# The first batch's last expert becomes the first slot of the second stage, its weights made in small pieces

## The chip, the core and the metric

The kernel runs on one core of one Trainium2 chip. The metric is the device time of one execution in microseconds (us); the figure for the kernel before is the median of three timed runs. A profile of one further execution shows where the time goes.

## The reference, cut to what matters

```
attn_out = attention(q, k, v, centroids)          # 4 batches, 8 heads, 768 rows, 64 wide
x = attn_out as [3072, 512]                       # 768 rows of each batch
P = balanced gates exp(x @ w_gate), 8 experts
for e in range(8):
    h = maximum(x @ w1[e], 0)                     # [3072,512] @ [512,1024]
    out += P[:, e:e+1] * (h @ w2[e])              # [3072,1024] @ [1024,512]
```

Only the mixture of experts is touched by the change; attention stands ahead of it and stays as it is.

## The kernel before, in words

**Two precisions.** Each fp32 matrix is split into a high and a low fp16 part, and each product is made of three matmuls (high by high, high by low, low by high). The first matrix product of an expert (`layer1`) is done with seven products in place of eight (Strassen's scheme in Winograd's form), 42 matmuls of 384 columns for a **quarter** of an expert, which is 256 of its 1024 hidden columns. An expert has four quarters. The weights of the seven products are four sums and three plain parts of `w1`, each in a high and a low part; they are made once and stored in DRAM (`w1d`).

**First stage: batch 0, 32 blocks.** The loop `for t in range(NI)` goes over the 8 x 4 quarters; I call one turn a *block* t. A block has seven steps m = 0 to 6. Each step makes one product of `layer1`, and from step 1 on one row tile of `layer2` of the quarter before: six matmuls of 512 columns, that is, the second matrix product in its plain form, 36 matmuls for a quarter. While block t runs, `make_w` makes the weights of quarter t+1 from the raw ones: ScalarE (ACT) scales and makes high parts, GpSimd (POOL) makes the four sums and the low parts of `w1`, VectorE (DVE) the low parts of `w2` (`second_matrix`, L1502). `scan` takes magnitudes of a later expert's raw weights for its scale. `store_w` writes the made weights to DRAM. The results of layer 2 collect in six PSUM tiles over the four blocks of an expert; `gated` adds them to `acc`, one 128x512 DVE instruction a tile (L1562), in the block after the expert's last one. Those blocks (t = 4, 8, 12, ...) I call *heavy*.

**Second stage: batches 1 to 3, 24 slots.** A *slot* is one expert of one batch, 28 steps. `layer1b` makes the first products, and `layer2b` the second products of the slot before, which here too are seven products in place of eight: 252 matmuls of 256 columns. The first slot has only `layer1b`, seven steps a quarter. The four sums of `w2` that the seven products need are made in the second stage's first eight slots: `load_second` (tile `r`), `second_sums` on POOL (`s2w`), `second_high` on ACT, `second_low` on DVE, with a store to `w2d`. `load_left` loads them back (tile `w2o`). `evict` gates results into the totals C11, C12, C21, C22 and X; at a batch's last expert POOL adds X to C12 and C22 (L1821), and the totals are stored as output.

**What sets the order.** Each engine executes its instructions in the order of the program. In the second stage a table of times (`at`, `plan_slot`) says in which step an instruction is issued; `keep_order` pins it. The engine that evicts matters to TensorE (PE): layer 1 has two PSUM tiles in turn, and a product can begin only when DVE or ACT has read what its tile held. In a block, what product 6 leaves must be read (L1401, tile `c`) before step 1 of the next block, which comes after one product only, since step 0 has no layer 2.

**Reload of x.** The seven input matrices of a batch's layer 1 (`xsB..`, `xsT..`, 384 KB each) have one buffer each. At a batch's last quarter `reload_x` loads the next batch's matrix as soon as the product that used the old one is done (L1381). All loads and stores that matter here are issued by SyncE (SP), one queue, in program order.

Of the kernel before, what the change touches and what calls it, by code (L numbers as in the profile page):

```python
# [22 lines left out]
P = 128  # L23
# [141 lines left out]
def attn_moe_kernel(  # L165
# [1116 lines left out]
    ps_h = pool("ps_h", 2, space=PSUM)  # L1282

    def h_tile():
        return ps_h.tile([P, 512], F32, name="h_ps")
# [35 lines left out]

    def spread_powers(am, n, name, use):

        d = dram.tile([P, n], F32, name=name)
        nc.sync.dma_start(out=d, in_=am)
        yield
        t = gs.tile([P, P, n], F32, name=f"all{n}", bufs=1)
# [126 lines left out]
    next(sink)  # L1454
    before = iter(())

    with ExitStack() as ax:
        hc = pool("hc", 4, ax)
        hp = pool("hp", 2, ax)
        wbp = pool("wbp", 3, ax)  # L1460
        sump = pool("sump", 1, ax)
        junkp = pool("junkp", 1, ax)
        rawp = pool("rawp", 8, ax)
        accp = pool("accp", 1, ax)
        ps_o = pool("ps_o", 6, ax, space=PSUM)
# [26 lines left out]
        def first_matrix(idx):  # L1492
            raw = raws[idx][:, 0:1024]
            return raw, raw.rearrange("p (k c t f) -> p t k c f", k=2, c=KC, t=2), sump.tile([P, 4, KC, P], F32, name="s1w")

# [35 lines left out]

        def store_w(idx, wt):
            e, f2 = divmod(idx, NP2)
            wa, wb = wt
            if idx > 1:
                nc.sync.dma_start(out=w1d[idx], in_=wa.rearrange("p x a c f -> p (x a c f)"))
            for o, t, h in ((A22, 0, 1), (A11, 1, 0), (A12, 0, 0)):
                nc.sync.dma_start(out=w2d[e][:, o, f2], in_=wb[:, :, t, h * HD : (h + 1) * HD])
# [14 lines left out]

        def gated(e, acc):
# [12 lines left out]

        AHEAD = 7
        wts = {}
# [7 lines left out]
        plan.unpin()  # L1577
        acc = accp.tile([P, NT, DO], F32, name="acc")
        scans = {i - 5: (i,) for i in range(8, NI)}
        loads = {0: (), 1: (4, 5), 2: (6, 7, 8), 3: (9, 10)}  # L1580
        loaded = {}
        for t in range(NI):
            e, f2 = divmod(t, NP2)
            if f2 == 0:
                po = []
            for idx in loads.get(t, (t + AHEAD,) if t + AHEAD < NI else ()):
                load_raw(idx)
            if 0 < t < NI - 1:
                wts[t + 1] = w_tiles()
                making = make_w(t + 1, wts[t + 1])  # L1590
            if t + 2 >= NI:
                loaded[t + 2] = load_wa((t + 2) % NI)
# [31 lines left out]
            for m in range(7):  # L1624
# [23 lines left out]
            wts.pop(t - 1, None)  # L1648
            before = layer2(po, hh, hl, wt, f2 == 0, f2 == NP2 - 1, gated(e, acc) if f2 == NP2 - 1 else None)
        for x in (sink, inputs, scanning):  # L1650
            for _ in x:
                pass
# [12 lines left out]
    hop = pool("hop", 6)  # L1665
    accp = pool("accb", 1)
    ps_y = pool("ps_y", 1, space=PSUM)
    slots = [(b, e) for b in range(1, B) for e in range(E)]
    NS = len(slots)
# [62 lines left out]
    def plan_slot(n):  # L1732
# [22 lines left out]
        at(base - 1, gate_slot, n)  # L1755
        if b == 1:
            first = base - SLOT
# [9 lines left out]
    LAST = {3: ("C11", 0, 0), 4: ("C22", 1, 1), 5: ("C12", 0, 1), 6: ("C21", 1, 0)}  # L1767
    totals = {}

    def evict(e, ps, gates_, into, begun, qs):  # L1770
        for q in qs:
            for name, j in into:
                t, gate = totals[name][:, q], gates_[:, 3 * j + q : 3 * j + q + 1]
                if e == 0 and (name, q) not in begun:
                    begun.add((name, q))
                    nc.vector.tensor_scalar(out=t, in0=ps[q], scalar1=gate, scalar2=None, op0=ALU.mult)
                else:
                    nc.vector.scalar_tensor_tensor(out=t, in0=ps[q], scalar=gate, in1=t, op0=ALU.mult, op1=ALU.add)

    def layer2b(n):  # L1780
# [6 lines left out]
        for i, (a, o) in enumerate(ORDER2):  # L1787
# [8 lines left out]
            for name, j in INTO[i]:  # L1796
                if name not in totals:
                    totals[name] = accp.tile([P, 3, HD], F32, name=name, bufs=2 if name == "C21" else 1)
            count = 0
            for g in range(2):  # L1800
                h = parts_.pop((n, g, o))
                for q in range(3):
                    steps = [(h_, w_, f) for f in range(2) for h_, w_ in ((0, 0), (0, 1), (1, 0))]
                    for s_, (h_, w_, f) in enumerate(steps):
# [100 lines left out]
```

## Time and profile before

| | |
|---|---|
| median of three timed runs | 2281.86 us (2281.69 to 2282.4) |
| the profiled execution's own time | 2279.16 us |
| its span, first to last instruction | 2277.1 us |
| attention, until the first block | 477.29 us |
| first stage (32 blocks and their rest) | 477.29 to 955.03 us |
| second stage (24 slots and their rest) | 955.03 to the end |
| granted TensorE clock, mean | 0.995 |

The profile lists for every engine its instructions with start, duration and what ended an idle time before them. Times in it are microseconds from the first instruction. A group of matmuls is shown with the time from its first start to its last (modelled) end, so the lengths of matmul groups that follow each other overlap a little; the distance of their starts is what counts.

### The profile page before, as it was taken

The page shows a single profiled execution, that of the slowest core. Times are in us where ns is not written, and L with a number is a line of the kernel's source. Part 1 is how long each engine was busy: PE and PEld are TensorE (multiplying, and loading weights), DVE is VectorE, ACT ScalarE, POOL GpSimd, SP SyncE. Part 2 cuts the span into 40 slices and gives each one's busy share as a digit, 9 for nine tenths or more (in the row PEclk, how much of TensorE's full clock was granted, in tenths as well). Part 3 has the DMA queues.
Part 4 walks back from the last instruction along what each step waited for, and adds up shares of the span by engine and source line. Part 5 has one row for each costly group of instructions (what it writes and reads, how often), then busy time and mean ns, then how long its engine had stood idle before and what let it go on. Part 6 is the DMA issues. An engine that isn't in the chain of part 4 may idle for free.

```text
span 2277.1 us, 39662 instructions
## 1 busy us (share of the span) xinstructions
PE 2236.1 (98%) x15491; PEld 1458.8 (64%) x15491; DVE 1649.1 (72%) x2777; ACT 1143.1 (50%) x2107; POOL 1118.1 (49%) x997
## 2 busy tenths in 40 slices
PE   6999999999999999999999999999999999999999
PEld 3455554445555555567777777777777777777777
DVE  7988878567666766588788877776676666666667
ACT  7777786555666665354444443333433333333333
POOL 3676787854555655276666653233332332322223
PEclk7999999999999999999999999999999999999999
DMA  5345453365555543586766765544444554434433
GB/s 128 88 101 159 103 142 98 124 218 198 186 168 190 190 139 111 203 300 210 223 218 218 239 219 169 176 144 132 151 156 141 182 170 139 131 130 132 138 130 102
DMA packets 226860, 369.78 MB, mean 162 GB/s; under 512 B 73800, under 2 KB 163824, under 8 KB 226160
## 3 DMA queue, kind: packets, MB, share of 16 engines
q1 hardware_dynamic: 226240, 365.67, 50.3%
q8 instruction: 121, 1.98, 0.4%
q10 hardware_dynamic: 432, 1.57, 0.2%
q14 instruction: 67, 0.55, 0.1%
HBM read 272.22 MB, written 80.62 MB: 155 GB/s over the span
## 4 chain that ended last, share of the span: by engine, by line
PE 91%; DVE 6%; ACT 2%; issue 1%; DMA 1%; SPq 0%; DVEq 0%; ACTq 0%
PE h_ps L1387 38%; PE pb L1805 12%; PE pa L1805 8%; PE pc L1805 8%; PE av_ps L1004 4%; PE o_ps L1547 4%; PE o_ps L1549 4%; PE o_ps L1548 4%; PE exp_ps L945 2%; PE max_ps L849 2%; PE exp_ps L946 2%; DVE mrt L853 2%; PE misc_ps L1045 1%; PE misc_ps L630 1%; ACT pe L952 0%
## 5 line engine op out<-in xcount | busy, mean ns | idle before, releaser
L1387 PEld LDWEIGHTS <-wa 128*128 128x128 f16 x5376 | 525.6, 98 | 302.8 <-issue 5.3
L1805 PEld LDWEIGHTS <-ho 128*128 128x128 f16 x5940 | 580.8, 98 | 137.2 <-DVE ho L1700 1.1
L1387 PE MATMUL h_ps<-xsT,wa 128*128 128x384 f16 x3072 | 581.6, 326 | 1.2 <-DVE xsT L324 0.6
L1387 PE MATMUL h_ps<-xsB,wa 128*128 128x384 f16 x2304 | 436.9, 326 | 1.4 <-DVE B L1401 0.6
L1681 POOL TENSOR_TENSOR B<-B,B 128x768 f32<-128x768 f32 x96 | 197.9, 2064 | 468.2 <-DVE ho L1700 426.6
L1700 DVE TENSOR_TENSOR ho<-B,ho 128x768 f16<-128x768 f32 x283 | 348.1, 1230 | 1.6 <-ACT ho L1696 1.6
L1851 ACT ACTIVATE B<-B 128x384 f32<-128x384 f32 x288 | 149.7, 520 | 371.3 <-DVE B L1401 370.0
L1805 PE MATMUL pb<-w2o,ho 128*128 128x256 f16 x2532 | 322.2, 273 | 0.0
L1401 DVE SCALAR_TENSOR_TENSOR u<-h_ps,m 128x384 f32<-128x384 f32 x256 | 141.7, 553 | 243.5 <-PE h_ps L1387 240.7
L1696 ACT CAST ho<-B 128x768 f16<-128x768 f32 x283 | 226.8, 824 | 14.1 <-POOL B L1681 13.4
L970 POOL TENSOR_TENSOR psum<-psum,pe 128x512 f32<-128x512 f32 x160 | 208.1, 1317 | 43.6 <-ACT pe L952 40.3
L853 DVE TENSOR_REDUCE mrt<-max_ps 128x1 f32<-128x512 f32 (+1 forms) x288 | 188.8, 683 | 41.0 <-PE max_ps L849 39.7
L1805 PE MATMUL pc<-w2o,ho 128*128 128x256 f16 x1692 | 215.7, 273 | 0.3
L1805 PE MATMUL pa<-w2o,ho 128*128 128x256 f16 x1692 | 215.1, 273 | 0.0
L1681 POOL TENSOR_TENSOR B<-B,T 128x768 f32<-128x768 f32 x48 | 95.6, 1991 | 206.0 <-DVE ho L1700 206.0
L952 ACT ACTIVATE pe<-exp_ps 128x512 f32<-128x512 f32 x288 | 164.8, 597 | 56.9 <-PE exp_ps L946 51.2
L1411 ACT ACTIVATE m<-h_ps 128x384 f32<-128x384 f32 x128 | 62.6, 489 | 191.6 <-PE h_ps L1387 190.8
L1849 ACT ACTIVATE B<-h_ps 128x384 f32<-128x384 f32 x96 | 47.1, 490 | 211.4 <-PE h_ps L1387 211.4
L1549 PE MATMUL o_ps<-wb,hl 128*128 128x512 f16 x384 | 145.5, 379 | 0.0
L1548 PE MATMUL o_ps<-wb,hh 128*128 128x512 f16 x384 | 145.5, 379 | 0.0
L1547 PE MATMUL o_ps<-wb,hh 128*128 128x512 f16 x384 | 145.5, 379 | 0.0
L1610 ACT ACTIVATE hh<-c 128x384 f16<-128x384 f32 x128 | 66.9, 523 | 143.2 <-DVE c L1401 142.0
(281 smaller groups left out, 3280.8 us busy)
## 6 DMA issues: line engine op xcount, KB each, us to landing
wa<-w1d SPq DMA_DIRECT2D x98, 896.0 KB
w2o<-w2d SPq DMA_DIRECT2D x168, 512.0 KB
raw<-in_moe_w SPq DMA_DIRECT2D x60, 512.0 KB
w1d<-wa SPq DMA_DIRECT2D x30, 896.0 KB
r<-in_moe_w SPq DMA_DIRECT2D x32, 512.0 KB
w2d<-w2s SPq DMA_DIRECT2D x32, 512.0 KB
w2d<-wb SPq DMA_DIRECT2D x96, 128.0 KB
scan<-in_moe_w SPq DMA_DIRECT2D x32, 256.0 KB
```

Of the source, the lines that this page charges most:

```text
L853: nc.vector.tensor_reduce(out=t["mr"][:, i0 : i0 + ni, ni - 1], in_=ps.rearrange("p (x c) -> p x c", x=ni), axis=AX, op=ALU.max)
L952: nc.scalar.activation(pe, ps.rearrange("p (x c) -> p x c", x=ni), AF.Exp, scale=SCALE)
L970: (nc.gpsimd if e == POOL else nc.vector).tensor_tensor(out=st[:, o : o + N0], in0=old[o], in1=part, op=ALU.add)
L1387: nc.tensor.matmul(ps[:, 0:HB], wa[:, w_, a, c, :], x[:, x_, c, :], start=(first and s_ == 0), stop=(s_ == len(steps) - 1), skip_group_che ...
L1547: nc.tensor.matmul(po[i], hh[:, t, ti], wbh[:, t], start=(first and t == 0), stop=False)
L1548: nc.tensor.matmul(po[i], hh[:, t, ti], wbl[:, t], start=False, stop=False)
L1549: nc.tensor.matmul(po[i], hl[:, t, ti], wbh[:, t], start=False, stop=(last and t == 1))
L1681: nc.gpsimd.tensor_tensor(out=t, in0=d[a], in1=d[c], op=ALU.subtract)
L1696: nc.scalar.copy(t[:, 0], blocks[n, g][o])
L1700: nc.vector.tensor_tensor(out=t[:, 1], in0=blocks[n, g][o], in1=t[:, 0], op=ALU.subtract)
L1805: nc.tensor.matmul(ps[q], h[:, h_, f, q * P : (q + 1) * P], w[:, 2 * g + f, w_], start=(first and g == 0 and s_ == 0 and q % 2 == 0), stop ...
L1851: rests.append(lambda: nc.scalar.activation(c, c, AF.Relu))
```

## The change

Batch 0's expert 7 (`STD = E - 1`) leaves the first stage and becomes slot 0 of the second. The first stage has 28 blocks, the second stage 25 slots. What goes with it:

- The four quarters' weights of expert 7 are still made in the first stage, but no longer by `make_w` in the block before. A generator `later` runs one step in every step of blocks from t = 2 on. It loads each half of a quarter (`w1` or `w2`, 512 KB) once for the magnitudes and once more for the weights, and makes each quarter by a fixed list of pieces, one or two a step, 26 steps from quarter to quarter. In that list the four sums are made by DVE (L333, four 128x256 instructions) instead of POOL.
- `acc` is gone: batch 0 now collects in the totals C11 to C22 as the other batches do, so a tile's eviction is two 128x256 DVE instructions in place of one 128x512.
- The reload of x for batch 1, in the last block before, now happens in the last quarter of slot 0.
- In the first stage there are six raw buffers in place of eight, loads go out six blocks ahead in place of seven, and `w2`'s made weights have four buffers in place of three. Output of batch 0 is stored by SP from the totals in slot 1, not by ACT at the end of the first stage.
- X begins anew in slot 0 (`n == 0`), and the adding of X and the stores of the batch's end now happen in slot 1 too.

```diff
+    STD = E - 1
...
-                if e == 0:
-                    nc.vector.tensor_scalar(out=acc[:, i], in0=ps, scalar1=gate, scalar2=None, op0=ALU.mult)
-                else:
-                    nc.vector.scalar_tensor_tensor(out=acc[:, i], in0=ps, scalar=gate, in1=acc[:, i], op0=ALU.mult, op1=ALU.add)
-                if e == E - 1 and i % 2 == 1:
-                    nc.scalar.dma_start(out=out_v[0][:, i - 1 : i + 1], in_=acc[:, i - 1 : i + 1])
+                j, q = divmod(i, 3)
+                for r, name in enumerate((("C11", "C21"), ("C12", "C22"))[j]):
+                    o, y = totals[name][:, q], ps[:, r * HD : (r + 1) * HD]
+                    if e == 0:
+                        nc.vector.tensor_scalar(out=o, in0=y, scalar1=gate, scalar2=None, op0=ALU.mult)
+                    else:
+                        nc.vector.scalar_tensor_tensor(out=o, in0=y, scalar=gate, in1=o, op0=ALU.mult, op1=ALU.add)
...
-        AHEAD = 7
+        AHEAD = 6
...
+        def later():
+            whole = [(e, f2, m) for e in range(STD, E) for f2 in range(NP2) for m in range(2)]
+            todo, ahead, spreads = whole + whole, [], []
...
+                return {
+                    0: [lambda: nc.scalar.activation(t1, t1, AF.Copy, scale=s1[:, e : e + 1])],
+                    2: [lambda: summed(0, 1)],
+                    3: [second_high],
+                    4: [lambda: summed(2, 3)],
+                    5: [plain_high],
+                    6: [lambda: second_low(0)],
+                    7: [lambda: plain_low(0)],
+                    8: [lambda: second_low(1), lambda: nc.scalar.copy(into["wa"][:, 0, 3:7], S_)],
+                    9: [lambda: plain_low(1)],
+                    11: [lambda: sum_low(0), fetch],
+                    12: [lambda: store_second(idx, into["wb"])],
+                    13: [lambda: sum_low(2), fetch],
+                    16: [lambda: store_first(idx, into["wa"])],
+                }
+
+            TURN = 26
...
-        for t in range(NI):
+        for t in range(NB):
...
+                if t > 1:
+                    step(extra)
                 if m:
                     step(before)
                 if m == 1:
                     store_w(t, wt)
-                if t == NI - 1:
-                    reload_x(1, RIGHT[m])
...
-    slots = [(b, e) for b in range(1, B) for e in range(E)]
+    slots = [(0, e) for e in range(STD, E)] + [(b, e) for b in range(1, B) for e in range(E)]
...
-        if b == 1:
+        if n < E:
...
-                if e == 0 and (name, q) not in begun:
+                if (e == 0 or n == 0 and name == "X") and (name, q) not in begun:
```

The first place is SP's queue in the second stage's first slot, around its last quarter. In names, `w2s` are made sums on their way to DRAM, `wa` the weights of layer 1, `w2o` those of layer 2, `r` raw `w2` for the next sums. Before:

```order
L1724 DMA w2d_6452<-w2s 128x4x512
L1343 DMA wa<-w1d_103 128x3584
L1704 DMA w2o<-w2d_6452 128x2048
L1708 DMA r_11459<-in_moe_w 128x2x512
L1708 DMA r_11496<-in_moe_w 128x2x512
L1343 DMA wa<-w1d_104 128x3584
L1704 DMA w2o<-w2d_6452 128x2048
```

And in the changed kernel:

```order
L1854 DMA w2d_6459<-w2s 128x4x512
L1346 DMA wa<-w1d_99 128x3584
L1384 DMA xsB_11030<-xsd1B_6467 128x1536
L1384 DMA xsT_11042<-xsd1T_6468 128x1536
L1384 DMA xsB_11053<-xsd1B_6470 128x1536
L1384 DMA xsT_11068<-xsd1T_6471 128x1536
L1834 DMA w2o<-w2d_6459 128x2048
L1838 DMA r_11073<-in_moe_w 128x2x512
L1384 DMA xsT_11083<-xsd1T_6469 128x1536
L1384 DMA xsT_11095<-xsd1T_6472 128x1536
L1384 DMA xsB_11108<-xsd1B_6473 128x1536
L1838 DMA r_11116<-in_moe_w 128x2x512
```

The seven loads of x now stand behind the store of sums and the load of `wa` of the slot's last quarter, and the loads of `r`, of `w2o` and of the next `wa` stand between or behind them.

The second place is DVE's order in block 16, a heavy one, steps 2 to 4 (`u` and `c` are layer 1's evictions, `xst` a part of the next batch's x, `hl` the low part of h). Before:

```order
L324 SCALAR_TENSOR_TENSOR xst<-tx,sx,xst 128x768
L1562 SCALAR_TENSOR_TENSOR acc<-o_ps,gates,acc 128x512
L1401 SCALAR_TENSOR_TENSOR u_8943<-h_ps,m_8882 128x384
L1613 SCALAR_TENSOR_TENSOR hl<-c,hh 128x384
L1562 SCALAR_TENSOR_TENSOR acc<-o_ps,gates,acc 128x512
L1401 SCALAR_TENSOR_TENSOR c<-h_ps,u_8943 128x384
```

And in the changed kernel, the same steps:

```order
L325 SCALAR_TENSOR_TENSOR xst<-tx,sx,xst 128x768
L333 TENSOR_TENSOR s1x<-rawx 128x256
L333 TENSOR_TENSOR s1x<-rawx,s1x 128x256
L1586 SCALAR_TENSOR_TENSOR C_6542<-o_ps,gates,C_6542 128x256
L1586 SCALAR_TENSOR_TENSOR C_6543<-o_ps,gates,C_6543 128x256
L1404 SCALAR_TENSOR_TENSOR u_9073<-h_ps,m_9004 128x384
L1744 SCALAR_TENSOR_TENSOR hl<-c,hh 128x384
L1586 SCALAR_TENSOR_TENSOR C_6542<-o_ps,gates,C_6542 128x256
L1586 SCALAR_TENSOR_TENSOR C_6543<-o_ps,gates,C_6543 128x256
L1404 SCALAR_TENSOR_TENSOR c<-h_ps,u_9073 128x384
L1658 SCALAR_TENSOR_TENSOR wb<-rawx,s_93,wb 128x512
```

Two sums and one low part of expert 7's weights have come between the evictions, and each eviction of layer 2 is two instructions.

## Rows read from the trace of the kernel before

**Rows 1.** The page: span, busy time by engine, the chain by engine.

```profile
span 2277.1 us, 39662 instructions
...
PE 2236.1 (98%) x15491; PEld 1458.8 (64%) x15491; DVE 1649.1 (72%) x2777; ACT 1143.1 (50%) x2107; POOL 1118.1 (49%) x997
...
PE 91%; DVE 6%; ACT 2%; issue 1%; DMA 1%; SPq 0%; DVEq 0%; ACTq 0%
```

**Rows 2.** Groups of PE's instructions: shape, count, busy, mean ns, idle before.

```profile
L1387 PE MATMUL h_ps<-xsT,wa 128*128 128x384 f16 x3072 | 581.6, 326 | 1.2 <-DVE xsT L324 0.6 <-DVE B L1401 0.4
...
L1805 PE MATMUL pb<-w2o,ho 128*128 128x256 f16 x2532 | 322.2, 273 | 0.0
...
L1549 PE MATMUL o_ps<-wb,hl 128*128 128x512 f16 x384 | 145.5, 379 | 0.0
```

**Rows 3.** Windows: blocks 8 to 27, slots 11 to 15, slot 0.

```profile
core 0: us, PE busy (x) PEld busy (x) DVE busy (x) ACT busy (x) POOL busy (x), PEclk, DMA share, GB/s
596.99:888.88 291.89, 291.89 (x1561) 152.65 (x1560) 189.95 (x314) 182.83 (x303) 160.39 (x164) 1.00 0.50 166
1532.73:1806.78 274.05, 274.05 (x2102) 205.48 (x2100) 184.49 (x310) 105.50 (x177) 82.80 (x43) 1.00 0.47 153
...
955.03:983.68 28.65, 27.69 (x169) 16.42 (x168) 17.97 (x26) 14.90 (x25) 17.61 (x21) 1.00 0.84 284
```

**Rows 4.** Timeline of PE in slot 0: its two waits [idle before <-releaser].

```profile
970.25 1.14 PE L1387 MATMUL h_ps<-xsT,wa 128*128 128x384 f16 x6 [0.36 <-DVE B L1401]
...
982.71 2.11 PE L1387 MATMUL h_ps<-xsB,wa 128*128 128x384 f16 x12 [0.60 <-DVE B L1401]
```

**Rows 5.** Timeline of SP: last reload of x; first and last of seven transfers.

```profile
946.16 0.32 SPq L1381 DMA_DIRECT2D xsB<-xsd1B  x1
...
969.76 0.36 SPq L1724 DMA_DIRECT2D w2d<-w2s  x1
...
978.53 0.46 SPq L1343 DMA_DIRECT2D wa<-w1d  x1
```

**Rows 6.** DMA issues, 930 to 990 us: count and KB each.

```profile
wa<-w1d SPq DMA_DIRECT2D x6, 896.0 KB
...
w2d<-w2s SPq DMA_DIRECT2D x4, 512.0 KB
xsT<-xsd1T SPq DMA_DIRECT2D x4, 384.0 KB
```

**Rows 7.** Windows of slot 0's end: last two columns are DMA share, GB/s.

```profile
970.00:975.00 5.00, 4.75 (x30) 2.86 (x30) 3.20 (x5) 2.48 (x5) 3.65 (x5) 1.00 0.99 315
975.00:980.00 5.00, 5.00 (x32) 3.00 (x31) 2.87 (x4) 4.31 (x8) 1.12 (x3) 1.00 1.04 393
980.00:985.00 5.00, 4.40 (x30) 2.65 (x28) 4.80 (x5) 1.99 (x4) 4.92 (x5) 1.00 1.00 316
```

**Rows 8.** Timeline of DVE, block 16, end of step 5 and step 6.

```profile
726.33 1.64 DVE L1502 SCALAR_TENSOR_TENSOR wb<-raw,s,wb 128x512 f16<-128x512 f32 x1
727.89 0.74 DVE L1562 SCALAR_TENSOR_TENSOR acc<-o_ps,gates,acc 128x512 f32<-128x512 f32 x1
728.55 0.54 DVE L1401 SCALAR_TENSOR_TENSOR c<-h_ps,u 128x384 f32<-128x384 f32 x1
...
729.48 0.74 DVE L1502 SCALAR_TENSOR_TENSOR wb<-raw,s,wb 128x512 f16<-128x512 f32 x1
```

**Rows 9.** Timeline of PE: block 17 begins, steps 0 and 1.

```profile
728.34 1.14 PE L1387 MATMUL h_ps<-xsB,wa 128*128 128x384 f16 x6
729.32 1.14 PE L1387 MATMUL h_ps<-xsT,wa 128*128 128x384 f16 x6
```

**Rows 10.** Timeline of POOL, block 16: the low parts of the sums.

```profile
724.83 2.59 POOL L1524 TENSOR_TENSOR wa<-s1w,wa 128x512 f16<-128x512 f32 x2 [1.63 <-ACT wa L1522]
```

**Rows 11.** Timeline of DVE in slot 1: pace of split evictions (start, length).

```profile
992.35 0.47 DVE L1776 TENSOR_SCALAR X<-pa,gates 128x256 f32<-128x256 f32 x1
992.75 0.47 DVE L1776 TENSOR_SCALAR C<-pa,gates 128x256 f32<-128x256 f32 x1
```

**Rows 12.** Timeline of POOL in slot 1: idle time; and POOL's adding of X.

```profile
1002.56 2.73 POOL L1681 TENSOR_TENSOR B<-B,T 128x768 f32<-128x768 f32 x1 [1.66 <-DVE ho L1700]
...
L1821 POOL TENSOR_TENSOR C<-C,X x6: 1807/1816/2519, 1378.5 to 2255.6; 128x768 f32<-128x768 f32 x6
```

More of the change, by code (lines that the diff above doesn't have):

```diff
@@ L1320, in gates, with spread_powers @@
             nc.vector.tensor_tensor(out=pr, in0=pr, in1=c2.unsqueeze(1).broadcast_to([P, NTT, E]), op=ALU.mult)
-    def spread_powers(am, n, name, use):
+    def spread_powers(am, n, name, use, own=""):
         d = dram.tile([P, n], F32, name=name)
@@ L1326, in spread_powers @@
         yield
-        t = gs.tile([P, P, n], F32, name=f"all{n}", bufs=1)
+        t = gs.tile([P, P, n], F32, name=f"all{n}{own}", bufs=1)
         nc.sync.dma_start(out=t, in_=d.partition_broadcast(P))
@@ L1455, in attn_moe_kernel, with total_tile @@
     before = iter(())
+    totals = {}
+    def total_tile(name):
+        return accp.tile([P, 3, HD], F32, name=name, bufs=2 if name == "C21" else 1)
     with ExitStack() as ax:
@@ L1493, in first_matrix @@
             raw = raws[idx][:, 0:1024]
-            return raw, raw.rearrange("p (k c t f) -> p t k c f", k=2, c=KC, t=2), sump.tile([P, 4, KC, P], F32, name="s1w")
+            return raw, raw.rearrange("p (k c t f) -> p t k c f", k=2, c=KC, t=2), sump.tile([P, 4, KC, P], F32, name="s1w" if idx < NB else "s1x")
         def second_matrix(idx, wb):
@@ L1532, in store_w, with store_first, store_second @@
         def store_w(idx, wt):
+            if idx > 1:
+                store_first(idx, wt[0])
+            store_second(idx, wt[1])
+        def store_first(idx, wa):
+            nc.sync.dma_start(out=w1d[idx], in_=wa.rearrange("p x a c f -> p (x a c f)"))
+        def store_second(idx, wb):
             e, f2 = divmod(idx, NP2)
-            wa, wb = wt
-            if idx > 1:
-                nc.sync.dma_start(out=w1d[idx], in_=wa.rearrange("p x a c f -> p (x a c f)"))
             for o, t, h in ((A22, 0, 1), (A11, 1, 0), (A12, 0, 0)):
@@ L1581, in attn_moe_kernel, with enumerate_quarter @@
+        def enumerate_quarter(i, idx, turn):
+            return [(i * turn + y * 1, (i, y)) for y in (0, 2, 3, 4, 5, 6, 7, 8, 9, 11, 12, 13, 16)]
+        extra = later()
+        for name in ("C11", "C21", "C12", "C22"):
+            totals[name] = total_tile(name)
+        loads = {0: (), 1: (4, 5), 2: (6, 7, 8), 3: (9,)}
         loaded = {}
-        for t in range(NI):
+        for t in range(NB):
             e, f2 = divmod(t, NP2)
@@ L1585, in attn_moe_kernel @@
                 po = []
-            for idx in loads.get(t, (t + AHEAD,) if t + AHEAD < NI else ()):
+            for idx in loads.get(t, (t + AHEAD,) if t + AHEAD < NB else ()):
                 load_raw(idx)
-            if 0 < t < NI - 1:
+            if 0 < t < NB - 1:
                 wts[t + 1] = w_tiles()
                 making = make_w(t + 1, wts[t + 1])
-            if t + 2 >= NI:
+            if t + 2 >= NB:
                 loaded[t + 2] = load_wa((t + 2) % NI)
@@ L1648, in attn_moe_kernel @@
             wts.pop(t - 1, None)
-            before = layer2(po, hh, hl, wt, f2 == 0, f2 == NP2 - 1, gated(e, acc) if f2 == NP2 - 1 else None)
-        for x in (sink, inputs, scanning):
+            before = layer2(po, hh, hl, wt, f2 == 0, f2 == NP2 - 1, gated(e) if f2 == NP2 - 1 else None)
+        for x in (sink, inputs, scanning, extra):
             for _ in x:
@@ L1767, in attn_moe_kernel, with evict @@
     LAST = {3: ("C11", 0, 0), 4: ("C22", 1, 1), 5: ("C12", 0, 1), 6: ("C21", 1, 0)}
-    totals = {}
-    def evict(e, ps, gates_, into, begun, qs):
+    def evict(n, e, ps, gates_, into, begun, qs):
         for q in qs:
@@ L1797, in layer2b @@
                 if name not in totals:
-                    totals[name] = accp.tile([P, 3, HD], F32, name=name, bufs=2 if name == "C21" else 1)
+                    totals[name] = total_tile(name)
             count = 0
```

106 lines of the change are left out of this document (91 added, 15 removed).

## The prediction, made before the run

> **What bounds the kernel now.** I read the page first: PE is busy 98% of the span and the chain that ended last runs 91% over PE [rows 1]. That alone says little, since matmuls overlap, so I looked at what PE waits for. The groups of PE show almost nothing: the largest layer-1 group has 1.2 us of idle time over 3072 matmuls, both forms of layer 2 have none [rows 2]. So from the first block on, the time is the number of matmuls by their pace, plus a few places where an eviction is late. The pace is read from windows between the starts of blocks and slots [rows 3]: 20 blocks take 291.89 us, 14.594 each, with PE busy all the time; 5 slots take 274.05 us, 54.81 each. Slot 0, which has layer 1 alone, takes 28.65 us and holds two waits of PE, 0.36 and 0.60 us, both for DVE's evictions [rows 4]. The granted clock is 1.00 in all of these windows.
>
> **What the change removes from PE.** Four blocks go, one slot comes: 4 x 14.594 = 58.38 against 54.81, that is 3.57 us less. All of it is layer 2: a block's plain 36 matmuls of 512 columns become a share of the seven products. Layer 1 stays, and so do the transition with layer 2 alone and the slot with layer 1 alone, each once before and after. If nothing else changes, this is the gain, and it is only 0.16% of the time. Whether the number is larger or smaller hangs on new waits of PE.
>
> **The reload of x.** Before, its seven loads went out in the last block and its rest, the last at 946.16, 8.87 us before slot 0 needs a tile at 955.03 [rows 5, 3]. Now they stand in slot 0's last quarter, whose seven products follow each other at 0.98 us (the distance of starts in [rows 9]) as no layer 2 lies between. And slot 1 needs the first tile right behind the seventh product, where slot 1 begins in the trace before, at 983.68 [rows 3]. In SP's queue the first x stands behind the load of `wa` issued at 978.53. What is queued then? Between the issues at 969.76 and 978.53 lie seven transfers [rows 5]: two `wa` of 896 KB, three stores of `w2d`, one `r` and one `w2o` of 512 KB each [rows 6], together 4352 KB or 4.46 MB. From 970 to 980 the DMA engines are full (share 0.99 and 1.04) and move 1.58 + 1.97 = 3.54 MB [rows 7]. The other 0.92 MB need 2.9 us at the 316 GB/s of the next window, so `wa` has landed at 982.9; up to an `r` of 512 KB from before 970 may be left over in part, I take 0.3 MB of it, and get to 983.9. The first x (384 KB, 0.39 MB) takes 1.0 to 1.24 us at 393 or 316 GB/s and is there at 984.9 to 985.1. [...] So PE waits from 983.68 to about 985.6: **2.0 us** lost. Bounds: nothing, if the queue drains faster than my account or x passes `wa`; 3.5 us, if the whole `r` is left over and each step goes at 316 GB/s. The other six tiles come at 1.0 to 1.24 us each, while PE, once layer 2 of slot 0 lies between the products, needs one only every 54.81 / 28 = 1.96 us; the first four come in a row, the next three with 1 MB more ahead of them (2.7 to 3.3 us), which the lead of four tiles covers. Behind x wait an `r`, a `wa` and two `w2o`; 7 x 0.39 = 2.75 MB ahead of them cost 7 to 9 us, and they are needed 8 us or more into slot 1. That is close; I set nothing for it and keep it for the range.
>
> **The end of batch 0 in slot 1.** POOL adds X to two totals, 1.82 us each, and idles 1.66 us in that place; PE's new wait gives it 2 us more [rows 12]. Nothing is set for it. If that cover is gone, POOL's sums come up to 2 us later and ACT, which waits for them, evicts later too.
>
> **The weights in the first stage.** Per quarter ACT gets five more pieces, DVE six, POOL four, and the same work is gone from blocks 27 to 30. Over blocks 8 to 27 ACT, DVE and POOL are busy 183, 190 and 160 of 292 us, the DMA share is 0.50 [rows 3]: room on average for all of it, the second load of every half too (16 loads of 512 KB where 8 were). Where it may cost is the place with the least room. In a heavy block DVE is behind at step 6: the eviction `c` ends at 728.55 + 0.54 = 729.09, PE uses that PSUM tile at 729.32 [rows 8, 9]. The room is 0.23 us. Splitting the eviction adds two instructions at a pace of 0.40 [rows 11] for one that held DVE 0.66 (727.89 to 728.55), so 0.14: 0.09 us are left in each of the blocks 4 to 24. The list of pieces starts 44 steps after block 2 begins and repeats every 26, so low parts (pieces 6 and 8) fall on step 4 just in blocks 16 and 20. Such a piece takes DVE 0.74 us alone and 1.64 us beside POOL's low parts [rows 8, 10]. If all of it moves the eviction, PE waits 0.74 - 0.09 = 0.65 us or 1.55 us; if it falls into idle time ahead of step 5, nothing. I take 0.35 in each, **0.7 us**, nearer to nothing, since DVE waits for PE in the steps before. In blocks 8 and 12 it is sums that stand in step 4; no row shows such a sum on DVE, its bounds are nothing and the 0.74 of a piece of twice its columns, and since POOL's slow part begins behind step 4 I set nothing.
>
> Why does a low part take 0.74 or 1.64? POOL's two instructions run from 724.83 to 727.42, and the slow one spans that end [rows 8, 10]. [...]
>
> **The sum.** -3.57 + 2.0 + 0.7 = -0.87 us. Against the profiled execution (span 2277.1, own time 2279.16, 2.1 us around the span) that is 2278.3; the median of the timed runs stands 2.7 us above the profiled one, and the difference goes onto the median: 2281.86 - 0.87 = **2281.0 us**. A measurement of this kernel can tell about 0.2% (4.6 us) from no change, so this is no change.
>
> **Rivals.**
> - The reload stays hidden, since the transfers ahead of it are done sooner. For it: before, nothing of slot 1 waited for a DMA though the engines were full. Against it: x is issued only some 5 us before it is needed, behind 4.46 MB. -3.57 + 0.7 = -2.9: 2279.0.
> - Faster: the two waits of slot 0 go as well, because the reload no longer fills the queue ahead of slot 0's loads and DVE and POOL run earlier there. -3.57 - 0.96 = -4.5, 2277.3 with the reload hidden. Against it: both waits are for DVE, not for a transfer [rows 4].
> - Slower: DVE falls behind in all seven heavy blocks. Place: the eviction at step 6, with its 0.23 us of room. If a split eviction costs like a whole one (0.66 more, 0.43 beyond the room) in seven blocks, and the pieces in four of them each add a POOL instruction's 1.3 us (half of 2.59, [rows 10]), it is 7 x 0.43 + 4 x 1.3 = 8.2 us. -3.57 + 2.0 + 8.2 = +6.6: 2288.5. It decides from 6.1 us on, 0.9 us in each heavy block. Against it: split evictions run at 0.40 [rows 11].
> - In between: DMA goes on late behind the reload, `r` and `w2o` too, or the heavy blocks cost half of that: +1.5 to +4.5, 2283.4 to 2286.4.
>
> **Chances.** As forecast (2279.7 to 2283.2): 0.55. Reload hidden: 0.15. Faster by more than 0.2%: 0.07. In between: 0.14. Slower rival or what comes to the same: 0.09. So faster by over 0.2% 0.07, within 0.2% 0.84, slower 0.09. The range goes from 2278.2 (reload hidden and nothing lost in the blocks: -3.57) to 2285.0 (the upper bounds of both losses, 3.5 + 2 x 1.55, come to +3.0): it leaves out the two outer cases and a part of the one in between.
>
> **What would show it.** Right: slot 1's first product waits 1 to 3.5 us with a load of `xsB` as what ended it; blocks of 14.6 us except 16 and 20; slots of 54.81. Wrong: no wait there; or blocks 8, 12, 16 and 20 of 15.5 us and more with DVE as the releaser; or ACT waiting for POOL's sums in slot 1 with PE behind it; or a first block that begins later than 477.29.

## The result, and the profile after

The changed kernel is slower: median 2309.14 us (2306.8 to 2310.06, four runs) against 2282.13 us (2281.69 to 2282.52, four runs) of the kernel before on the same chip, a ratio of 1.0115 [1.0099, 1.0131]. The forecast was 2281.0 us, its range ended at 2285.0. The page of the profile after, which answers to [rows 1]:

```profile
span 2305.0 us, 39975 instructions
...
PE 2245.0 (97%) x15599; PEld 1472.0 (64%) x15599; DVE 1680.4 (73%) x2855; ACT 1145.4 (50%) x2109; POOL 1124.3 (49%) x991
...
PE 84%; DVE 8%; DMA 4%; ACT 2%; issue 1%; SPq 1%; POOL 0%; DVEq 0%; ACTq 0%
```

The busy shares say nothing of 27 us; the chain that ended last does. PE's part fell from 91 to 84%, and DMA, which had 1%, has 4%: 4% of 2305 is some 90 us in which the chain runs over a transfer, some 70 more than before. Not all of that is lost, since PE can be busy beside a transfer that the chain follows. Where is time lost? I measured the distance from each block's first layer-1 matmul to the next block's. The span grew by 27.9 us, and this is where:

| place | before | after | difference |
|---|---|---|---|
| four blocks less, a slot more | 4 x 14.594 | 54.81 | -3.57 |
| blocks 7, 8, 11, 15, 19 | 14.60 each | 17.00, 16.77, 20.95, 16.81, 20.32 | +18.85 |
| blocks 14, 17, 20, 21 | 14.60 each | 14.88, 15.16, 15.14, 15.25 | +2.0 |
| block 3 | 15.29 | 16.09 | +0.8 |
| slots 0 and 1 | 28.65, 55.09 | 32.41, 57.93 | +6.6 |
| start of block 0, and block 0 | 477.29, 14.65 | 479.39, 15.81 | +3.3 |

All other blocks and slots are as before. Two things had not been forecast at all: blocks 7 to 19, and what follows the wait for x.

**Block 11.** The view of waits names what DVE and PE waited for (us in total, times, longest):

```profile
DVE gmax L1335 <- DMA all<-amw: 17.9, 4, 5.7
...
PE h_ps L1390 <- DVE u L1404: 11.0, 4, 4.7
```

`gmax` belongs to a chain that my working did not have: `spread_powers`. Once per expert the partial magnitudes `am`, two in each of 128 partitions (1 KB), are stored to DRAM (`amw`), read back to every partition (`all`, 128 KB), and DVE takes the largest and makes the expert's scale of it. Every step waits for the one ahead. In block 10 of the kernel before, SP issued this (start, length):

```profile
627.43 0.91 SPq L1538 DMA_DIRECT2D w2d<-wb  x2
634.24 0.33 SPq L1325 DMA_DIRECT2D amw<-am  x1
637.15 0.33 SPq L1328 DMA_DIRECT2D all<-amw  x1
```

For 6 us nothing had been issued ahead of `amw`; it landed after 2.9 us and let `all` go. DVE came to `gmax` in its own order at 643.54. That left almost nothing in hand: by the landing reports in the trace (the updates of its semaphore), the last part of `all` came at 643.22. In blocks 15 and 19 of the kernel before DVE did wait for `all`, 0.60 and 0.76 us, and PE lost nothing by it. The view of waits before had it in one line:

```profile
DVE gmax L1332 <- DMA all<-amw: 1.4, 2, 0.8
```

In the changed kernel the same place looks like this:

```profile
637.86 0.37 SPq L1489 DMA_DIRECT2D raw<-in_moe_w  x1
638.28 0.50 SPq L1490 DMA_DIRECT2D raw<-in_moe_w  x1
638.82 1.59 SPq L1559 DMA_DIRECT2D w2d<-wb  x3
640.52 0.52 SPq L1484 DMA_DIRECT2D rawx<-in_moe_w  x1
641.13 0.65 SPq L1554 DMA_DIRECT2D w1d<-wa  x1
641.83 2.36 SPq L1559 DMA_DIRECT2D w2d<-wb  x3
644.29 1.14 SPq L1328 DMA_DIRECT2D amw<-am  x1
645.52 0.73 SPq L1554 DMA_DIRECT2D w1d<-wa  x1
652.55 0.32 SPq L1331 DMA_DIRECT2D all<-amw  x1
```

Within 6.4 us ahead of `amw` SP issues two `raw` and a `rawx` of 512 KB, a `w1d` of 896 KB and six `w2d` of 128 KB, 3.2 MB in all. The 1 KB takes 8.3 us (644.29 to 652.55) in place of 2.9. Behind it, ahead of `all`, comes another 896 KB. What that does to DVE and PE:

```profile
651.71 0.55 DVE L1744 SCALAR_TENSOR_TENSOR hl<-c,hh 128x384 f16<-128x384 f32 x1
657.87 0.42 DVE L1335 TENSOR_REDUCE gmax<-all 128x2 f32<-128x256 f32 x1 [5.62 <-DMA all<-amw]
...
659.19 0.55 DVE L1404 SCALAR_TENSOR_TENSOR u<-h_ps,m 128x384 f32<-128x384 f32 x1
```

```profile
654.72 0.38 PE L1570 MATMUL o_ps<-wb,hl 128*128 128x512 f16 x1
659.79 2.08 PE L1390 MATMUL h_ps<-xsT,wa 128*128 128x384 f16 x6 [4.70 <-DVE u L1404]
661.66 0.63 PE L1568 MATMUL o_ps<-wb,hh 128*128 128x512 f16 x1
```

The eviction `u` stands behind `gmax` on DVE, and PE behind `u`. After 4.70 us of waiting PE's six matmuls take 2.08 us where they took 1.14: the granted clock (third column from the end) is 0.50 from 660.00 to 662.50, where the kernel before has 1.00. That is the rest of the block's 6.35 us.

```profile
660.00:662.50 2.50, 2.50 (x8) 1.03 (x7) 0.59 (x2) 2.47 (x7) 2.00 (x3) 0.50 1.02 382
```

The other long blocks have the same wait of DVE: two in block 7 (the second, at its end, for expert 7's own chain, `all2x`), one each in blocks 15 and 19.

```profile
590.58 0.42 DVE L1335 TENSOR_REDUCE gmax<-all 128x2 f32<-128x256 f32 x1 [2.43 <-DMA all<-amw]
601.53 0.42 DVE L1335 TENSOR_REDUCE gmax<-all2x 128x2 f32<-128x256 f32 x1 [5.04 <-DMA all2x<-amw]
720.25 0.42 DVE L1335 TENSOR_REDUCE gmax<-all 128x2 f32<-128x256 f32 x1 [4.12 <-DMA all<-amw]
783.24 0.42 DVE L1335 TENSOR_REDUCE gmax<-all 128x2 f32<-128x256 f32 x1 [5.71 <-DMA all<-amw]
```

Block 8 begins right behind the second one. PE waits 0.46 us more there for DVE's `c` and then runs at a granted clock of 0.50 (605 to 607). At 16.77 us with DVE as the releaser it looks like a sign of the slower rival, but what made DVE late is its wait of 5.04 us for `all2x`.

**Slots 0 and 1.** PE waits for x, as forecast, but 4.0 us:

```profile
948.94 1.14 PE L1390 MATMUL h_ps<-xsB,wa 128*128 128x384 f16 x6 [0.21 <-DVE B L1404]
954.06 2.08 PE L1390 MATMUL h_ps<-xsB,wa 128*128 128x384 f16 x6 [3.99 <-DMA xsB<-xsd1B]
```

And behind the wait the granted clock is low, where [rows 3, 7] showed 1.00 throughout:

```profile
950.31:955.00 4.69, 0.94 (x4) 0.45 (x5) 3.68 (x4) 0.83 (x1) 4.61 (x3) 0.79 1.01 400
955.00:960.00 5.00, 5.00 (x21) 2.83 (x20) 0.00 (x0) 1.94 (x3) 4.29 (x3) 0.52 1.03 412
960.00:1012.00 52.00, 51.86 (x400) 38.78 (x399) 41.41 (x59) 22.22 (x35) 30.88 (x25) 1.00 0.73 253
```

PE counts as busy for all 5 us from 955 on, at a mean granted clock of 0.52. Slot 1 takes 2.8 us more than before.

### The profile page after: what moved, and what is told of

Read it like the earlier page. It is cut to its first block, busy times and chain, and to the rows that moved or that the text cites. A ratio compares the mean times of both kernels' runs of the same rounds, so it can differ in the third digit from the quotient of the medians.

```text
span 2305.0 us, 39975 instructions
## 1 busy us (share of the span) xinstructions
PE 2245.0 (97%) x15599; PEld 1472.0 (64%) x15599; DVE 1680.4 (73%) x2855; ACT 1145.4 (50%) x2109; POOL 1124.3 (49%) x991
## 4 chain that ended last, share of the span: by engine, by line
PE 84%; DVE 8%; DMA 4%; ACT 2%; issue 1%; SPq 1%; POOL 0%; DVEq 0%; ACTq 0%
PE h_ps L1390 35%; PE pb L1934 13%; PE pa L1934 9%; PE pc L1934 8%; PE av_ps L1005 4%; PE o_ps L1568 2%; PE o_ps L1569 2%; PE o_ps L1570 2%; DVE mrt L854 2%; PE exp_ps L946 2%; PE max_ps L850 2%; PE exp_ps L947 2%; DMA amw<-am 1%; DMA all<-amw 1%; PE misc_ps L1046 1%
## 5 line engine op out<-in xcount | busy, mean ns | idle before, releaser
L1934 PEld LDWEIGHTS <-ho 128*128 128x128 f16 x6192 | 606.0, 98 | 144.2 <-DVE ho L1830 1.6
L1811 POOL TENSOR_TENSOR B<-B,B 128x768 f32<-128x768 f32 x100 | 206.6, 2067 | 497.5 <-DVE ho L1830 454.3
L1830 DVE TENSOR_TENSOR ho<-B,ho 128x768 f16<-128x768 f32 x295 | 363.6, 1233 | 2.5 <-ACT ho L1826 2.5
L1934 PE MATMUL pb<-w2o,ho 128*128 128x256 f16 x2640 | 335.9, 273 | 0.0
L1826 ACT CAST ho<-B 128x768 f16<-128x768 f32 x295 | 236.5, 824 | 13.4 <-POOL B L1811 12.7
L1934 PE MATMUL pc<-w2o,ho 128*128 128x256 f16 x1764 | 225.0, 273 | 0.5
L1934 PE MATMUL pa<-w2o,ho 128*128 128x256 f16 x1764 | 225.3, 273 | 0.0
L1404 DVE SCALAR_TENSOR_TENSOR B<-h_ps,u 128x384 f32<-128x384 f32 x200 | 110.4, 552 | 47.2 <-PE h_ps L1390 46.3
L1005 PE MATMUL av_ps<-pe,vn 128*64 128x512 f32 (+1 forms) x768 | 134.4, 492 | 0.0
L1568 PE MATMUL o_ps<-wb,hh 128*128 128x512 f16 x336 | 128.4, 382 | 0.0
L1569 PE MATMUL o_ps<-wb,hh 128*128 128x512 f16 x336 | 128.3, 382 | 0.0
```

Of the source, the lines that this page charges most:

```text
L1005: nc.tensor.matmul(av[o, a:z], vn[:, i, :], heads[t]["pe", c][:, i - i0], start=(i == 0), stop=False, skip_group_check=True)
L1404: nc.vector.scalar_tensor_tensor(out=t, in0=ps[:, 0:HB], scalar=KAPPA, in1=x, op0=ALU.mult, op1=ALU.add)
L1568: nc.tensor.matmul(po[i], hh[:, t, ti], wbh[:, t], start=(first and t == 0), stop=False)
L1569: nc.tensor.matmul(po[i], hh[:, t, ti], wbl[:, t], start=False, stop=False)
L1811: nc.gpsimd.tensor_tensor(out=t, in0=d[a], in1=d[c], op=ALU.subtract)
L1826: nc.scalar.copy(t[:, 0], blocks[n, g][o])
```

## Experiments

Theory A: the scale chain comes late, because the change puts megabytes ahead of its two small transfers. Rival B, the slower rival of the prediction: DVE has too much work of its own. Apart from these, the price of x's wait. A plain block takes 14.60.

| kernel | us, median (runs) | ratio to before [95%] | blocks 7, 8, 9 | blocks 11, 15, 19 | slots 0, 1 |
|---|---|---|---|---|---|
| shift14 | 2289.19 (10) | 1.0030 [1.0020, 1.0039] | 17.35, 15.21, 15.18 | 14.60, 14.60, 14.60 | 32.57, 56.18 |
| scale_act | 2312.08 (4) | 1.0132 [1.0116, 1.0147] | 18.44, 18.93, 14.60 | 18.62, 19.54, 20.96 | 32.34, 57.59 |
| sums_pool | 2309.81 (1) | - | 17.88, 15.21, 15.24 | 21.85, 17.76, 20.48 | 32.20, 56.39 |
| x_ahead | 2301.77 (4) | 1.0085 [1.0070, 1.0101] | 16.29, 15.21, 15.19 | 20.50, 17.27, 20.33 | 28.90, 55.60 |
| x_act | 2305.61 (4) | 1.0100 [1.0085, 1.0115] | 16.42, 15.21, 14.71 | 21.96, 18.90, 20.20 | 28.54, 61.12 |
| both | 2285.30 (10) | 1.0012 [1.0003, 1.0022] | 17.38, 15.21, 14.89 | 14.60, 14.60, 14.60 | 28.83, 55.17 |
| spread7 | 2280.65 (10) | 0.9996 [0.9986, 1.0005] | 14.60, 14.60, 14.59 | 14.60, 14.60, 14.60 | 28.61, 55.16 |
| best | 2281.43 (11) | 0.9994 [0.9985, 1.0002] | 14.60, 14.60, 14.60 | 14.60, 14.60, 14.60 | 29.42, 55.60 |
| before_loads | 2280.94 (10) | 0.9999 [0.9989, 1.0008] | 14.60 each | 14.60, 14.60, 14.60 | 28.31, 54.81 |
| before_stores1 | 2282.07 (1) | - | 14.60 each | 14.77, 15.20, 14.84 | 28.23, 54.81 |
| before_stores3 | 2305.62 (1) | - | 14.60 each | 22.62, 22.13, 21.46 | 28.23, 54.81 |
| before_again | 2283.20 (1) | - | 14.60 each | 14.60, 14.60, 14.60 | 28.14, 54.81 |

**shift14.** The list of pieces starts 14 steps later, half an expert.

```diff
-                yield from wait(8)
+                yield from wait(22)
```

> The list of pieces begins 14 steps later, so that the loads and stores of a quarter of expert 7 fall between two scale chains (the am, amw, all, gmax of one expert each) in place of onto them; the DVE pieces then fall into the blocks of the chains. Theory A, the scale chain's two small transfers are late because big ones stand ahead of them: blocks 11, 15 and 19 go from 20.95, 16.81 and 20.32 back to within 0.6 us of 14.60, blocks 7 and 8 stay at 17.0 and 16.8 since nothing moves there; 14 to 16 us gained, median 2293 to 2295. Rival B, VectorE has too much work in these blocks: they stay late or get later, 2305 to 2312.

Blocks 11, 15 and 19 are back to 14.60, and by the medians 20 us are gone, more than expected. From block 1 to the end the two profiles differ by 18.1 us: 14.3 in those three blocks, 2.0 in blocks 14, 17, 20 and 21, and 3.2 in block 8 and slots 0 and 1 together, where PE waited about as long as in the changed kernel but ran less time at the lower clock; blocks 7, 9 and 13 give 1.4 back. The remaining 2 us need not be a gain of the edit: the profiled execution of the changed kernel lay 2.3 us under its median. In block 10 SP issues `amw` and `all` 5.7 us apart, and DVE comes to `gmax` without a wait, although two sums now stand right ahead of it:

```profile
642.52 0.33 SPq L1328 DMA_DIRECT2D amw<-am  x1
648.25 0.33 SPq L1331 DMA_DIRECT2D all<-amw  x1
```

```profile
651.36 0.41 DVE L333 TENSOR_TENSOR s1x<-rawx 128x256 f32<-128x256 f32 x1
651.70 0.41 DVE L333 TENSOR_TENSOR s1x<-rawx,s1x 128x256 f32<-128x256 f32 x1
652.03 0.54 DVE L1744 SCALAR_TENSOR_TENSOR hl<-c,hh 128x384 f16<-128x384 f32 x1
652.50 0.40 DVE L1335 TENSOR_REDUCE gmax<-all 128x2 f32<-128x256 f32 x1
```

So DVE has time for the pieces in the very blocks that were late; B falls for them.

**sums_pool.** `nc.vector` becomes `nc.gpsimd` in `summed`, nothing else.

> The changed kernel with the four sums of expert 7's weights on POOL in place of DVE, nothing else moved. If DVE's added work makes blocks 11, 15 and 19 late: they drop by 2 us or more each, 6 us in all. If it is the scale chain's transfers: they stay within 1 us of 20.95, 16.81 and 20.32, and only the small waits at the ends of heavy blocks (blocks 17, 20, 21, together 1.75 us over 14.60) get less.

The long blocks stay long. The small ones answer in part: block 17 goes from 15.16 to 14.65 and block 20 from 15.14 to 14.60, block 21 stays at 15.30. That DVE term is real, and small.

**scale_act.** ACT issues the chain's two transfers.

```diff
+        queue = nc.scalar if name.startswith("amw") else nc.sync
-        nc.sync.dma_start(out=d, in_=am)
+        queue.dma_start(out=d, in_=am)
...
-        nc.sync.dma_start(out=t, in_=d.partition_broadcast(P))
+        queue.dma_start(out=t, in_=d.partition_broadcast(P))
```

> The two small transfers of each first-stage scale chain (amw and all) are issued by ACT in place of SP, all else as in the changed kernel. Theory A1, they are late because they queue behind megabytes in SP's queue: the waits of DVE for all (17.9 and 5.0 us) go to under 3 us in all, blocks 7, 8, 11, 15, 19 come back to 14.6 to 15.2, median 2290 to 2293. A2, the 16 DMA engines are full and it doesn't matter which queue: less than half of that, 2299 to 2306. Rival B, VectorE's own work: no change, 2307 to 2311.

A1 fell. On a queue with nothing ahead of it `amw` takes as long:

```profile
648.32 0.33 ACTq L1328 DMA_DIRECT2D amw<-am  x1
...
656.46 0.33 ACTq L1331 DMA_DIRECT2D all<-amw  x1
```

8.1 us from one issue to the other, and it is the transfer that takes them: ACT has nothing to compute from 652.26 on, and `amw`'s last landing report comes at 656.38. So it was not the place in SP's queue. What the DMA engines had been given before shows in their share, 0.99 from 645 to 650 and 1.15 from 650 to 655; how transfers of SP's queue hold up one of ACT's is not shown. And ACT now stands in these waits, 8.7 us of them ahead of `xst`, so some blocks get longer. The median alone, 2312.08, would have spoken for B (2307 to 2311); it is shift14 and sums_pool that refute it.

**before_loads.** The kernel before, with six idle loads of 512 KB in blocks 10, 14 and 18.

```diff
+        dummy = pool("dummy", 3, ax)
...
+                if t in (10, 14, 18) and m in (1, 2):
+                    for i in range(3):
+                        x = dummy.tile([P, 1024], F32, name="dummy")
+                        nc.sync.dma_start(out=x.rearrange("p (c f) -> p c f", c=NC), in_=w1[e, :, 0 : 2 * P].rearrange("(c p) f -> p c f", p=P))
```

> The kernel before, with nothing of the change, but with six loads of 512 KB that nobody reads ahead of the scale chain in blocks 10, 14 and 18. If the bytes ahead of the small transfers are the cause: 3 MB at some 390 GB/s are 8 us, about 3 us of which the chain has in hand, so blocks 11, 15 and 19 take 3 to 6 us longer each, with PE waiting for DVE's u and DVE for all; 9 to 18 us in all, 2291 to 2300. If it needs the change's DVE work or split evictions: 14.60 each, 2282.

Nothing happened, and not because A is wrong: the loads waited for next to nothing, so SP issued them ahead of time, the last three from 629.21 on, and when `amw` went out at 635.01 the engines were done with them (DMA share 1.04 in the 2.5 us before, 0.24 in the 2.5 behind; `amw` took 3.0 us). Order in the program wasn't what counted here, either; time was. The next two make the big transfers wait for the same scan as the chain.

**before_stores1 and before_stores3.** One or three stores of the scanned raw tile (1 MB each).

```diff
+            if f2 == NP2 - 1 and e in (3, 4, 5):
+                nc.sync.dma_start(out=dram.tile([P, 1024], F16, name=f"spare{e}"), in_=junk)
+                for i in range(3):
+                    nc.sync.dma_start(out=dram.tile([P, 2048], F32, name=f"spare{e}_{i}"), in_=raws[idx])
```

> The kernel before with nothing of the change, but in blocks 10, 14 and 18 SP stores 1.25 MB (the scan's junk, then the scanned raw tile) to spare DRAM just ahead of the scale chain; the first of them waits for the scan as the chain does, so that they can't be gone before it. DVE has 9.3 us from am to the place of gmax (634.2 to 643.5 in before), the chain alone takes about 6. If the bytes ahead count: 1.3 MB at 390 GB/s add 3.4 us, just as much as is in hand: blocks 11, 15 and 19 take 14.6 to 15.6. If not: 14.60.

> The same with 3.25 MB ahead of the chain. If the bytes ahead count: 3.4 MB at 390 GB/s are 8.7 us, 5 to 6 more than are in hand: DVE waits about 5 us for all in each, blocks 11, 15 and 19 take 3 to 6 us longer, with the half clock behind it, as in the changed kernel. If it takes the change's own work on DVE: 14.60 each.

1.25 MB cost 0.17, 0.60 and 0.24 us, 3.25 MB cost 8.0, 7.5 and 6.9. With no part of the change in it, the kernel before becomes nearly as slow as the changed one; 22.4 us of it are in these three blocks. My expectation had the chain alone at about 6 us, with 3 in hand; by the landing reports it took 9.0 (634.24 to 643.22) with 0.3 in hand, and the 1.25 MB still cost only 0.2 to 0.6. DVE waited 0.94, 2.52 and 2.16 us at `gmax`, so 0.8 to 1.9 us of DVE's wait did not reach PE. SP's queue in block 10 of before_stores3, and its row among the waits:

```profile
637.61 0.33 SPq L1486 DMA_DIRECT2D spare<-junk  x1
637.99 2.07 SPq L1488 DMA_DIRECT2D spare<-raw  x3
640.16 1.19 SPq L1325 DMA_DIRECT2D amw<-am  x1
649.44 0.32 SPq L1328 DMA_DIRECT2D all<-amw  x1
```

```profile
DVE gmax L1332 <- DMA all<-amw: 20.8, 3, 7.6
```

**x_ahead.** In slot 0's last quarter the load of `wa` goes behind the seven x.

```diff
-            if q + 2 < B * NI:
+            held = n == 0 and f2 == NP2 - 1
+            if q + 2 < B * NI and not held:
                 loaded[q + 2] = load_wa((q + 2) % NI)
...
                     reload_x(b + 1, RIGHT[m])
+                    if held and m == 6:
+                        loaded[q + 2] = load_wa((q + 2) % NI)
```

> In slot 0's last quarter the load of wa (896 KB) that stands ahead of the seven x is issued behind them. If x is late because of what is queued ahead of it: 896 KB at some 390 GB/s is 2.4 us, so the wait before slot 1 goes from 4.0 to about 1.6 us, and with it some of the half clock behind it: 2.4 to 5 us, median 2304 to 2307. If the four x loads that run together hold up the first one (the engines out of step): under 1 us gained, 2308 to 2309.

The wait goes from 3.99 to 0.38 us, more than the 2.4 of those 896 KB: SP also comes to the first x sooner, 5.0 us ahead of its use (944.29) in place of 3.9 (946.15). And the clock stays up: behind the wait PE's six matmuls take 1.14 us, 2.08 in the changed kernel. Slots 0 and 1 take 84.50 us in place of 90.34:

```profile
948.18 1.14 PE L1390 MATMUL h_ps<-xsB,wa 128*128 128x384 f16 x6 [0.31 <-DVE B L1404]
949.69 1.14 PE L1390 MATMUL h_ps<-xsB,wa 128*128 128x384 f16 x6 [0.38 <-DMA xsB<-xsd1B]
950.66 1.15 PE L1934 MATMUL pa<-w2o,ho 128*128 128x256 f16 x9
```

**x_act.** `reload_x` issues batch 1's loads by `nc.scalar`.

> The seven x loads of slot 0 are issued by ACT in place of SP. If x waits for its turn in SP's queue: x is there before slot 1 needs it or up to 1 us late, 4 to 7 us gained, median 2302 to 2305. If the DMA engines, which are full there, are the limit: the wait stays 3 to 4 us, 2308 to 2310, or wa and w2o come late in its place.

Slot 1 begins without a wait for x, and then loses more: PE waits 4.48 us for ACT's `m`. In ACT's order that `m` stands behind its own DMA issues; two of them take 1.86 us, and from 952.03 to the issue at 956.12 ACT does nothing.

```profile
949.29 1.86 ACTq L1384 DMA_DIRECT2D xsT<-xsd1T  x2
951.20 0.83 ACT L1826 CAST ho<-B 128x768 f16<-128x768 f32 x1 [2.26 <-DMA w2o<-w2d]
956.12 0.36 ACTq L1384 DMA_DIRECT2D xsT<-xsd1T  x1
```

What held the issue at 956.12 the profile doesn't show for certain. x_act gains 0.7 us in the two slots, x_ahead 5.8.

**before_again.** The kernel before, a second profile.

> The kernel before, once more with a profile, to see what differs between two runs of one kernel. In the changed kernel and its four variants attention ends at 478.58 to 480.60 us and block 0 takes 15.81 to 16.93, against 477.29 and 14.65 in the one profile of before. If that is variation of runs: this one ends attention anywhere from 477 to 480.5 and block 0 takes 14.6 to 16.9. If it belongs to the change (its other layout of SBUF): 477.0 to 477.6 and 14.65 again.

It is variation of runs. Attention ends at 479.67, and block 0 takes 17.16 us at a mean granted clock of 0.80, against 14.65 at 1.00 in the first profile:

```profile
479.67:496.83 17.16, 13.99 (x81) 6.51 (x81) 13.06 (x22) 8.86 (x16) 1.41 (x2) 0.80 0.69 238
```

So the last row of the table on the 27.9 us need not come from the change.

**both, spread7, best.** `both` joins shift14 and x_ahead. `spread7` holds three loads back that came just ahead of expert 2's chain and lets expert 7's own chain go on in every fourth step only. `best` takes the magnitudes of expert 7's `w2` by ACT.

```diff
-                        fetch()
+                        if len(todo) > len(whole):
+                            fetch()
...
-                yield from wait(22)
+                for n in (8, 4, 4):
+                    yield from wait(n)
+                    fetch()
+                yield from wait(6)
...
-                for _ in range(n):
-                    for s in spreads:
-                        step(s)
+                for i in range(n):
+                    if i % 4 == 0:
+                        for s in spreads:
+                            step(s)
...
-                        if m:
-                            largest(am[:, m, f2 : f2 + 1], t)
-                        else:
-                            total(am[:, m, f2 : f2 + 1], t, junkp.tile([P, 1024], F16, name="junk"))
+                        total(am[:, m, f2 : f2 + 1], t, junkp.tile([P, 1024], F16, name="junk"))
```

> The 14 steps' shift and the load of wa behind the seven x together. If the two causes are apart from each other, the gains add: 2309.1 - 19.9 - 7.3 = 2281.9 us, within 2 us. If the one hid part of the other (the clock, the queue): 2285 or more.

> As both, and the scale chains of blocks 7 and 8 are cleared too: the three loads of raw weights that come last before block 7 wait until 8 steps behind expert 7's scale chain, and that chain advances every fourth step in place of each. If DVE's waits for the small transfers are the cause there too: blocks 7, 8 and 9 go from 17.35, 15.21 and 15.18 to 14.6 to 14.8, 3 to 4 us less than both, 2278 to 2279. If they come from DVE's scans or split evictions: as both, 2281 to 2283.

> As spread7, and the magnitudes of expert 7's raw w2 are taken by ACT (as those of its w1) in place of DVE. If the four scans of DVE are what makes csum late in block 3: block 3 goes from 16.08 to 15.29, and with block 13 still 0.48 over, the stretch from block 1 to the end is 3.57 - 0.48 = 3.1 us shorter than before, 2279 to 2280. If ACT's scans make another eviction late: blocks 2 to 6 lose 0.3 us or more in place of it, 2280 to 2282.

`both` came out 3.4 us over the sum of the gains, where its second alternative begins. From block 1 to the end the profiles gained 18.1 us in shift14, 7.5 in x_ahead and 22.8 in `both`, 2.7 less than the sum. Both single gains hold block 8's 1.56 us and 1.6 us of slots 0 and 1, lost at the lower clock, and these can be gained only once. `spread7` has one wait of `gmax` left, of 0.28 us, and from block 4 on only block 13 of the plain blocks is long (15.08). It changes two things at once, so how much each gave is not shown. `best` takes block 3 from 16.08 to 15.29, as expected, but x comes later there (a wait of 1.17 us, slots of 29.42 and 55.60), and its median isn't lower. From block 1 to the end the two take 1782.8 and 1783.2 us, the kernel before 1785.2 and 1784.5 in its two profiles: 1.3 to 2.4 us of the 3.57 are there. The medians can't tell either of them from the kernel before.

## Why the prediction was wrong

**The step that failed** is "room on average for all of it, the second load of every half too". It set the first stage's transfers at nothing by a DMA share of 0.50 [rows 3], and then looked for the place with the least room on DVE alone. But it isn't the engines that lacked room. A chain of two dependent small transfers has to come back within 9.3 us (`am` at 634.21, `gmax` at 643.54); it took 9.0 of them before the change, and how long it took hung on the bytes given to the DMA engines in the few microseconds ahead of it: from `amw` to `all` 2.9 us with nothing issued for 6 us ahead, 9.3 behind 3.25 MB. The dose (before_stores1 and 3) and the shift show that; the rival of more DVE work is refuted for the long blocks by shift14 and sums_pool. The price was 18.85 us in five blocks, of which shift14 gave back blocks 11, 15 and 19, and spread7 blocks 7 and 8.

That it hit just these: the list starts 44 steps into block 2 and repeats every 26; the chains stand 28 apart. Loads and stores of pieces 11 to 16 of the first three quarters therefore fall on or up to nine steps ahead of a chain. In the fourth quarter nothing is loaded, nor are raw weights in block 22, and block 23 is 14.60. The raw loads, six blocks ahead in six buffers in place of seven in eight, came nearer to the chain as well: block 10's pair went out 19.8 us ahead of `amw` before (614.44), 6.7 in shift14 (635.83), where `amw` and `all` are 5.7 us apart, 2.9 before. That alone does not make the blocks long, as shift14 has it and loses nothing in blocks 11, 15 and 19; no run changes the buffers alone.

**The reload of x**: the mechanism was right (a load of `xsB` ended the wait, behind the `wa` in SP's queue), the size was off. 4.0 us were measured for 2.0, a little over the upper bound of 3.5. From the issue of `wa` to the end of PE's wait the forecast had 7.1 us (978.53 to 985.6); it took 8.5 (945.60 to 954.06), and that `wa` went out 4.5 us ahead of x's use in place of 5.2. The half microsecond between the first x's landing (985.1) and 985.6 is shown by no run: the load's last landing report comes at 953.93 and PE starts 0.13 us behind it. What ran over is the spread of the landing: the load's sixteen reports come from 951.24 to 953.93, 5.6 to 8.3 us behind the issue of `wa`, where the forecast had 6.6 for all of it. And the low clock behind the wait, 2.8 us in slot 1, had no term. Together slots 0 and 1 lost 6.6 us for 2.0.

**Heavy blocks**: DVE's `c` was late at the ends of blocks 16 and 20, as forecast, for 0.7 us; measured 0.56 and 0.65 (blocks 17 and 21), and 0.8 more in blocks 14 and 20, which had no term. The places were right, the size a little over half of the 1.2 measured there. The mechanism holds at most for one of them: with the sums on POOL block 17 goes to 14.65, so its loss hung on DVE's sums, which I had set at nothing, and not on the low parts that I priced; so did block 20's. Block 21 stays long (15.30) with the low part in place; that it is the low part is not shown, and block 14's 0.28 is open. That a piece adds a POOL instruction's 1.3 us, as in the slower rival's sum, is shown by no run: the eight low parts of expert 7 took DVE 0.74 to 1.71 us in the changed kernel, 0.87 in the median, so at most 0.98 over the shortest. Block 3's 0.8 us was missed: DVE's scans make `csum` late there, as best shows.

**Right** were the structure (slots behind slot 1 as before, plain blocks of 14.60), POOL's adding of X, and the loads behind x: with the other causes gone slot 1 takes 55.16 (spread7) against 55.09 before. A first block later than 477.29, which I had named as a sign against me, was none: before_again.

## What to carry to other kernels

A share of busy DMA engines over a stage told of bytes here, not of delay: at 0.50 over blocks 8 to 27 the chain in block 10 had 0.3 us in hand. Look for small transfers on which a compute engine waits in its order, and count the bytes issued in the microseconds ahead of each; a change that adds traffic is placed between them, not on them. And three waits of PE cost more than their length here, by the low clock behind them (0.50 to 0.52): 4.7 + 1.65 us in block 11, 3.9 + 1.8 in block 19, 4.0 + 2.8 ahead of slot 1. It wasn't a fixed price: ahead of slot 1 in shift14 it was 4.25 + 1.4, and in block 8 waits of 1.72 and 0.46 us were followed by 1.6 us of it in the changed kernel, by none in shift14 after 1.77 and 0.46.

## What the runs showed of the hardware

- The 1 KB of `amw` took 2.9 us from its issue to that of `all` with nothing issued for 6 us ahead of it (before), 8.3 behind 3.2 MB (after), 9.3 behind 3.25 MB of stores (before_stores3, 640.16 to 649.44), and still 8.1 from ACT's queue, in which nothing stood ahead of it (scale_act, 648.32 to 656.46).
- Some issues took longer than others: SP's `amw` 1.14 us in the changed kernel, at a DMA share of 1.14 (644.0 to 645.5), 0.33 in the kernel before at 0.03 (634 to 637); in x_act two of ACT's x took 1.86 us together, the other five 0.33 to 0.36 each. A high share alone did not make them long: ACT's `amw` in scale_act took 0.33 at 0.99.
- Two executions of one program differed by 2.4 us at the end of attention and by 2.5 in block 0, the latter at a granted clock of 1.00 or 0.80; PE's first four waits in it were 0.57, 0.93, 0.35 and 0.34 us at 1.00, 0.57, 0.92, 0.35 and 0.34 at 0.80.
